# Moving three loads of values behind a later gate in a fused attention and feed-forward kernel

## The chip, the cores and the metric

The kernel runs on one core of one Trainium2 chip. The metric is the device time of one execution in microseconds (us); the lower the better. Runs of the kernel before give the time to compare with, and one further execution was taken with the hardware profiler.

## What is computed

The first stage is attention over a sliding window: eight batches, eight heads, 576 positions, heads of 64. A position sees the positions at most 32 away. The second stage takes the attention's output as 4608 tokens of 512 and runs a feed-forward block of width 2048 with a sigmoid-approximated GELU.

```python
scores = scale * np.matmul(q, k.transpose(0, 1, 3, 2))
mask = np.abs(pos[:, None] - pos[None, :]) <= window        # window = 32
attn = softmax(np.where(mask, scores, -1e9))
x = np.matmul(attn, v)                                      # (8, 8, 576, 64) -> (4608, 512)
h = x @ w_in                                                # (512, 2048)
g = h * (1.0 / (1.0 + np.exp(-1.702 * h)))
out = g @ w_out                                             # (2048, 512)
```

## The kernel before

The 4608 tokens are cut into 36 units of 128 and nine tiles of 512, four units to a tile. Units and tiles are counted from 0, so the third tile has the number t = 2, and while its first layer is computed, the attention of the units of the next tile is prepared. The whole order of work is written out by hand; each engine runs its own instructions strictly in the order in which the program issues them.

**Attention of a unit.** Queries and keys are loaded from memory into staging tiles (`qst`, `kst`, five buffers each, `load_kq`, L138), transposed by DMA from SP's queue (`T_dma`, L246, called by `turn`, L868) into `qT` and `kT`, multiplied to scores on the matrix engine (TensorE, called PE in the profile), turned into exponentials on ScalarE (ACT) and multiplied with a mask on VectorE (DVE; `band`, L360). The queries of a unit are shifted by 32 positions against its keys, so one half of the query rows needs the unit's own 128 values, and the other half the 128 values that begin 64 later.

**Values.** `load_v(u)` (L209) loads unit u's values into one of nine buffers `ve`, by a DMA issued from GpSimd (POOL). `odd_v(u)` (L224) makes the shifted copy `vo` of unit u, the "odd" values: one GpSimd copy takes the upper half of `ve` of unit u, a second the lower half of `ve` of unit u + 1. All loads of queries, keys and values are issued by GpSimd too, so the issues and the copies share one queue. `values_four(u)` (L407) multiplies the exponentials of four units with `ve` and `vo`, head after head, 32 heads in all (`pv` in the profile). `norm_four` (L425) divides by the sums on VectorE and sends each unit's result x to SP, which transposes it by DMA into `xT` of the next tile (L447).

**Feed-forward.** Both layers use Strassen-like schemes of seven products. `l1_group(t, n, ...)` computes group n of the four groups of the first layer of tile t; the products of the second layer of earlier tiles are kept in a list `l2` and filled in between. VectorE makes sums of the inputs (`xs`, L495 and L496, from `xT`) and of the results (`gs`, L507 to L510).

**The order around the change.** `back(t)` (L904) runs the four groups of tile t. At its start a group turns queries and keys on SP; in group 2 `values_four` and `norm_four` of the next tile's units take their place; the store of an output pair (L613, on SP) and the fill products are spread between. Behind each group stands a gate: GpSimd copies one element of the last sum `gs` into `seen` (L943), and as its queue is in order, it issues nothing further before VectorE has made that sum. Behind the gate GpSimd runs a row of the table `LOADS`, looked up by tile and group, else by group alone. In a row, `("v", 5)` loads the values of unit u + 5, `("kq", 9)` the queries of unit u + 9 and the keys of the unit after, and `("odd", 4)` makes the odd copies of unit u + 4, with u = 4t + 4, so u = 12 for the third tile. Values 17, 18 and 19 are one DMA each. `front(t)` (L877) stands between the tiles: the scores of the next tile's units, and the sums of x.

Of the kernel before, what the change touches and what calls it, by code (L numbers as in the profile page):

```python
# [26 lines left out]
class _Kernel:  # L27
# [689 lines left out]
    def opening(self):  # L717
# [95 lines left out]
        for u in (8, 9, 10, 11):  # L813
# [29 lines left out]
        self.x_T2(6, "t", act)  # L843
        self.do(self.l2, 5)

    LOADS = {(2, 1): [("kq", 8)], (2, 2): [("v", 5, 6, 7)], (2, 3): [("v", 8), ("kq", 9), ("odd", 4), ("kq", 10)],
# [25 lines left out]
    @staticmethod  # L872
    def do(fs, n=99):
        for _ in range(min(n, len(fs))):
            fs.pop(0)()
# [28 lines left out]
    def back(self, t):  # L904

        more = t + 1 < self.NT
        do, l2 = self.do, self.l2
        u = 4 * t + 4
        bands = [lambda i=i: self.band(u + i) for i in range(4)] if more else []
        dv = bands  # L910
        for n in range(4):
            for i in {2: ((4,), (5,), (6, 7), ()), 3: ((4, 5), (6, 7), (), (8,))}.get(t, ((5, 6), (7,), (), (8,)))[n]:
                self.turn(u + i)
            if t == 2:
                self.ahead("kq", *((17,), (18, 19), (), ())[n])
            if more and n == 2:
                self.values_four(u)
                self.norm_four(u, ("A", "C", "E"), (0, 1))
                do(l2, 1)

            key = n if more else ("last", n)
            if t == 2:
                key = ("first", n) if n < 2 else n
            share = dict(zip((1, 7, 2, 4), self.SHARES.get(key, (3, 3, 5, 5))))

            def fill(i):
                do(l2, share[i])
                self.l2eng = self.nc.scalar
                if i == 4 or more and (n, i) == (1, 7):
                    do(dv, 99 if i == 4 else 2)  # L930

            def side(i):
                if more and n == 2:
                    self.norm_four(u, (f"t{i}",), (2 + i,))
                else:
                    do(dv, 1)

            self.l1_group(t, n, fill, side)
            dv += self.g_sums(t, 2 * n, 2)
            if more and (t > 2 or n > 0):  # L940
                if u + n + 7 <= self.NU:
                    c = 2 * ((n - 1) % 4) + 1
                    self.nc.gpsimd.tensor_copy(self.seen, self.gs[t - (n == 0)][0:1, 2, c, 255:256])  # L943
                for what, *us in self.LOADS.get((t, n)) or self.LOADS[n]:
                    for i in us:
                        if what == "odd":
                            self.spread(u + i)
                        else:
                            self.ahead(what, u + i)
        return dv  # L950
# [136 lines left out]
```

## Time and profile before

| what | us |
|---|---|
| median of three timed runs | 279.52 |
| lowest and highest of them | 279.24, 280.18 |
| the profiled execution | 278.88 |
| its span, first to last instruction | 277.1 |
| TensorE busy in it | 265.1 |
| VectorE, ScalarE, GpSimd busy in it | 213.7, 196.1, 140.2 |

All times below that stand alone, such as 99.74, are us from the start of the span of the profiled execution. In a row of a timeline the first number is the start, the second the duration, then come the engine, the line of the kernel, the operation, what it writes and reads, and a count of merged instructions; a bracket tells how long the engine was idle before and what ended that. SPq is SP's queue of DMA issues. "To landing" is the time from a DMA's issue to the arrival of its data, as minimum, median and maximum. A row of a window has the window, its length, then for PE, weight loads, VectorE, ScalarE and GpSimd the busy us with the number of instructions, then the granted clock, the mean number of DMA engines' worth of queued work, and GB/s.

### The profile page before, as it was taken

What the parts mean: (1) busy time and instruction counts of PE and PEld (TensorE: products, weight loads), DVE (VectorE), ACT (ScalarE), POOL (GpSimd) and SP (SyncE); (2) the same over time, 40 slices, a digit from 0 to 9 for tenths busy, and PEclk for the clock granted to TensorE, in tenths of its full rate; (3) what the DMA queues carried; (4) which work ended last, traced back from release to release, by engine and by line L of the source; (5) the groups of instructions that cost most, each with busy time, mean ns of one, the idle gap of its engine ahead of it and who ended that gap; (6) DMA issues with size and microseconds to landing.
All of it is one profiled execution on the core that took longest, in us unless ns stands there. A gap on an engine that the chain in (4) does not pass through costs nothing.

```text
span 277.1 us, 8812 instructions
## 1 busy us (share of the span) xinstructions
PE 265.1 (96%) x3604; PEld 222.4 (80%) x3604; DVE 213.7 (77%) x496; ACT 196.1 (71%) x346; POOL 140.2 (51%) x218
## 2 busy tenths in 40 slices
PE   1989999999999999999999999999999999999994
PEld 1568556888788888888888888888888888888883
DVE  4655998987888788888878887888788878856621
ACT  2586985999896689669956985698569766577320
POOL 8995597999693189729642974294430000000000
PEclk9999999999999999999999999999999999999999
DMA  8999999999999999999999999999992023202033
GB/s 86 165 199 199 180 207 166 164 150 149 188 133 212 163 122 165 173 198 120 171 171 172 151 167 181 134 141 125 153 120 80 0 89 65 78 0 78 0 117 116
DMA packets 151353, 37.74 MB, mean 136 GB/s; under 512 B 138640, under 2 KB 146960, under 8 KB 151312
## 3 DMA queue, kind: packets, MB, share of 16 engines
q0 software_dynamic: 107200, 18.42, 95.4%
q1 hardware_dynamic: 43664, 18.23, 34.3%
q8 instruction: 28, 0.46, 0.7%
q10 hardware_dynamic: 448, 0.52, 0.6%
q14 instruction: 13, 0.11, 0.1%
HBM read 36.83 MB, written 9.44 MB: 167 GB/s over the span
## 4 chain that ended last, share of the span: by engine, by line
PE 93%; ACT 2%; DMA 2%; DVE 1%; issue 1%; POOLq 0%
PE o L71 41%; PE h L71 40%; PE sc L71 5%; PE pv L71 4%; DMA kq<-in_k_dram 2%; PE tp L180 1%; PE tp L259 1%; ACT kq L68 1%; PE tp L463 1%; ACT p L340 1%; DVE xn L398 1%; ACT L803 0%; PE tp L204 0%; DVE kq L68 0%; PE tp L451 0%
## 5 line engine op out<-in xcount | busy, mean ns | idle before, releaser
L579 ACT ACTIVATE g<-h 128x512 f16<-128x512 f32 x128 | 72.1, 598 | 37.9 <-PE h L71 31.6
L71 PEld LDWEIGHTS <-g 128*128 128x128 f16 x568 | 54.6, 98 | 7.7
L71 PE MATMUL h<-xs,a 128*128 128x256 f16 x384 | 57.6, 272 | 0.0
L71 PEld LDWEIGHTS <-a 128*128 128x128 f16 x512 | 49.7, 98 | 8.4 <-DVE xs L495 0.3
L71 PE MATMUL h<-xT,w 128*128 128x256 f16 (+1 forms) x352 | 53.6, 283 | 0.0
L71 PEld LDWEIGHTS <-w 128*128 128x128 f16 x480 | 46.0, 98 | 8.6
L71 PE MATMUL o<-w,g 128*128 128x256 f16 (+1 forms) x304 | 49.9, 284 | 0.0
L233 POOL COPY vo<-ve 64x264 int32<-64x264 int32 x71 | 35.6, 502 | 18.0 <-DMA ve<-in_v_dram 14.5
L71 PEld LDWEIGHTS <-gs 128*128 128x128 f16 x416 | 39.9, 98 | 5.3
L71 PE MATMUL o<-b,gs 128*128 128x256 f16 x280 | 43.3, 273 | 0.0
L71 PE MATMUL o<-b,g 128*128 128x256 f16 x264 | 38.6, 273 | 0.0
L592 DVE TENSOR_TENSOR h<-h,s 128x512 f32<-128x512 f32 x32 | 22.4, 699 | 18.8 <-PE h L71 18.2
L214 POOL DMA_DIRECT2D ve<-in_v_dram x39 | 33.2, 864 | 2.5 <-issue 1.2
L144 POOL DMA_DIRECT2D qst<-in_q_dram x35 | 28.2, 808 | 1.3 <-issue 0.9
L598 DVE TENSOR_TENSOR h<-h,s 128x512 f32<-128x512 f32 x32 | 22.3, 698 | 7.3 <-PE h L71 7.1
L144 POOL DMA_DIRECT2D kst<-in_k_dram x31 | 26.6, 861 | 1.4 <-DMA w<-in_moe_w_out_dram 1.4
L68 ACT COPY h<-h 128x512 f32<-128x512 f32 x32 | 18.8, 587 | 10.4 <-PE h L71 9.6
L293 ACT ACTIVATE p<-sc 128x512 bf16<-128x512 f32 x48 | 24.7, 623 | 0.3 <-PE sc L71 0.2
L943 POOL COPY seen<-gs 1x1 f16<-1x1 f16 x17 | 3.3, 196 | 36.9 <-DVE gs L510 36.9
L68 ACT COPY o_sb<-o 128x256 f32<-128x256 f32 (+1 forms) x25 | 11.7, 467 | 12.6 <-PE o L71 12.6
L68 ACT COPY s<-h 128x512 f32<-128x512 f32 x32 | 19.1, 598 | 0.8
L71 PE MATMUL h<-xs,w 128*128 128x256 f16 x128 | 19.2, 273 | 0.0
(101 smaller groups left out, 389.0 us busy)
## 6 DMA issues: line engine op xcount, KB each, us to landing
out_dram<-o_sb SPq DMA_DIRECT2D x33, 256.0 KB, 4.1
ve<-in_v_dram POOLq DMA_DIRECT2D x31, 128.0 KB, 6.5
kst<-in_k_dram POOLq DMA_DIRECT2D x25, 128.0 KB, 5.7
qst<-in_q_dram POOLq DMA_DIRECT2D x21, 128.0 KB, 5.2
w<-in_moe_w_out_dram POOLq DMA_DIRECT2D x4, 512.0 KB, 10.6
w<-in_moe_w_in_dram POOLq DMA_DIRECT2D x4, 256.0 KB, 8.5
w<-in_moe_w_in_dram POOLq DMA_DIRECT2D x2, 512.0 KB, 10.6
qst<-in_q_dram POOLq DMA_DIRECT2D x7, 96.0 KB, 5.8
```

What stands on the lines that cost most here:

```text
L68: (eng.copy if eng is self.nc.scalar else eng.tensor_copy)(out, in_)
L71: self.nc.tensor.matmul(out, lhsT, rhs, start=start, stop=stop, skip_group_check=True)
L144: self.nc.gpsimd.dma_start(t[off:off + n], src[b, :, s:s + n, :].rearrange("h s d -> s h d"))
L180: self.nc.tensor.transpose(tp[64 * (h % 2):64 * (h % 2) + 64, h // 2, x, :], src[:, 4 * i + h, at + x, :], self.ident[r, r])
L214: self.nc.gpsimd.dma_start(t[off:off + n, :, :self.D], self.v[b, :, s:s + n, :].rearrange("h s d -> s h d"))
L233: eng.tensor_copy(*((words(vo[64:128]), words(self.ve[u % 9][64:128])), (words(vo[0:64]), words(nxt)))[i])
L259: self.nc.tensor.transpose(tp[:, i, hp, :], src[:, 128 * hp:128 * hp + 128], self.ident)
L293: exps = [lambda eo=eo: self.nc.scalar.activation(p[:, eo].rearrange("k h s -> k (h s)"), sc[eo], AF.Exp, scale=self.scale) for eo in rang ...
L579: act.activation(g[:, f, 256 * half:256 * half + 256], bank.rearrange("p (i n) -> p i n", i=2), AF.Gelu_apprx_sigmoid)
L592: dve.tensor_add(e, b, s7)
L598: dve.tensor_add(c, b, s7)
L943: self.nc.gpsimd.tensor_copy(self.seen, self.gs[t - (n == 0)][0:1, 2, c, 255:256])
```

## The change

The row of the third tile's third group, (2, 2), becomes empty, and values 17, 18 and 19 go into the row of the fourth group, (2, 3), ahead of values 20. The lookup takes an empty row as a row: before, an empty one would have fallen through to the default of its group.

```diff
-    LOADS = {(2, 1): [("kq", 8)], (2, 2): [("v", 5, 6, 7)], (2, 3): [("v", 8), ("kq", 9), ("odd", 4), ("kq", 10)],
+    LOADS = {(2, 1): [("kq", 8)], (2, 2): [], (2, 3): [("v", 5, 6, 7, 8), ("kq", 9), ("odd", 4), ("kq", 10)],
              (3, 0): [("kq", 7), ("odd", 1, 2, 3), ("v", 5)],
              0: [("odd", 2), ("kq", 7), ("v", 5), ("odd", 3)], 1: [("kq", 8), ("v", 6)],
              2: [("odd", 4), ("kq", 9), ("v", 7)], 3: [("odd", 5), ("kq", 10), ("v", 8)]}
...
-                for what, *us in self.LOADS.get((t, n)) or self.LOADS[n]:
+                for what, *us in self.LOADS.get((t, n), self.LOADS[n]):
```

## The prediction, made before the change was run

> **What bounds the kernel now.** I read the page first, then the windows around the place of the change, then GpSimd's own order of time, and last the consumers of what GpSimd makes. On the page, the span, the busy times and the chain that ended last:
>
> ```profile
> span 277.1 us, 8812 instructions
> ...
> PE 265.1 (96%) x3604; PEld 222.4 (80%) x3604; DVE 213.7 (77%) x496; ACT 196.1 (71%) x346; POOL 140.2 (51%) x218
> ...
> PE 93%; ACT 2%; DMA 2%; DVE 1%; issue 1%; POOLq 0%
> ```
>
> The matrix engine is both the busiest engine and 93% of the chain. A busy share is an average, so the windows come next: I cut the stretch from the values of the third tile (87.30) in alternate pieces, from values to scores and from scores to values. The first column is the length, the second the matrix engine's busy time and its matmuls.
>
> ```profile
> 87.30:98.84 11.54, 11.54 (x162) 10.02 (x166) 9.44 (x25) 6.97 (x14) 4.57 (x6) 1.00 1.40 176
> 98.84:114.72 15.88, 15.88 (x232) 13.88 (x234) 13.69 (x29) 13.87 (x24) 13.10 (x21) 1.00 2.14 163
> 114.72:126.26 11.54, 11.54 (x162) 10.04 (x166) 9.49 (x25) 6.91 (x13) 6.13 (x10) 1.00 1.49 172
> 126.26:142.14 15.88, 15.88 (x232) 13.88 (x234) 13.58 (x29) 13.87 (x24) 9.77 (x17) 1.00 1.96 154
> ```
>
> This table decides most of the question. The first two pieces hold the loads that the change moves; the last two are the same work one tile later, where the change moves nothing. The lengths agree to 0.01 us (11.54 and 11.54, 15.88 and 15.88), with the same count of matmuls, a busy time equal to the length, and a clock of 1.00. So before the change no load, copy or transpose in this stretch makes the matrix engine wait, and a better place for a load has nothing to give back there. A change of GpSimd's order can only leave the time as it is, or add a wait.
>
> **The change part by part.** GpSimd's timeline, with the idle time ahead of an instruction in brackets:
>
> ```profile
> 95.72 0.18 POOL L943 COPY seen<-gs 1x1 f16<-1x1 f16 x1 [6.44 <-DVE gs L510]
> 96.19 2.63 POOL L214 DMA_DIRECT2D ve<-in_v_dram  x3 [0.29 <-issue]
> 99.74 0.24 POOL L943 COPY seen<-gs 1x1 f16<-1x1 f16 x1 [0.92 <-DVE gs L510]
> 100.25 0.88 POOL L214 DMA_DIRECT2D ve<-in_v_dram  x1 [0.27 <-issue]
> ...
> 103.42 1.18 POOL L233 COPY vo<-ve 64x264 int32<-64x264 int32 x2
> ...
> 107.78 0.89 POOL L144 DMA_DIRECT2D kst<-in_k_dram  x1
> 108.71 3.77 POOL L233 COPY vo<-ve 64x264 int32<-64x264 int32 x6
> ...
> 114.27 0.18 POOL L943 COPY seen<-gs 1x1 f16<-1x1 f16 x1 [0.97 <-DVE gs L510]
> ...
> 123.14 0.18 POOL L943 COPY seen<-gs 1x1 f16<-1x1 f16 x1 [5.23 <-DVE gs L510]
> ```
>
> The gate of the third group (the copy into `seen` at 95.72) stays, since it stands ahead of the row of loads and does not depend on it. The edit of the lookup adds no instruction: it lets an empty row count as a row. So nothing is added or removed; the three issues of values 17 to 19 are moved past one gate, the one at 99.74. That gate waits for VectorE and was already idle by 0.92 us before it, so it does not come earlier when the three issues are gone from ahead of it. From 100.25 on, everything in GpSimd's queue up to the last copy stands three issues later, which is 2.63 us: values 20, queries 21 and 22, keys 22 and 23, the two copies of odd unit 16, the gate of the next tile, queries 23, keys 24, and the six copies of odd units 17 to 19. Between 100.25 and the end of these copies (108.71 + 3.77 = 112.48) the queue has next to no gap (of its 2.78 idle us in the window from 98.84, 0.90 lie before the gate, 0.27 behind it and 0.97 before 114.27), so nothing there takes up the shift: the copies would end at 112.48 + 2.63 = 115.11 if each cost what it cost before.
>
> Do they cost the same? The six took 3.77 us, 0.63 each, beside VectorE's long mask products, the last of which end at 110.7. The row of these, and the group of all copies of this kind from 111.3 on, later in the same kernel:
>
> ```profile
> 109.20 1.49 DVE L367 TENSOR_TENSOR p<-p,mask 128x1024 bf16<-128x1024 bf16 x2
> ...
> L233 POOL COPY vo<-ve 64x264 int32<-64x264 int32 x29 | 13.6, 469 | 9.8 <-DMA ve<-in_v_dram 8.4
> ```
>
> At 0.469 us six take 2.8, and the end is 115.11 - 3.77 + 2.8 = 114.1. I keep both: 114.1 to 115.1, nearer the first, because at the new place the mask products are over. Who needs them? The products of values with odd units in the same phase, in the matrix engine's timeline (the first of 32, and the 25th, which is the first of unit 19, eight heads to a unit):
>
> ```profile
> 114.65 0.22 PE L71 MATMUL pv<-vo,p 128*64 128x65 bf16 x1
> ...
> 115.47 0.19 PE L71 MATMUL pv<-vo,p 128*64 128x65 bf16 x1
> ```
>
> Unit 19 is wanted at 115.47, 0.4 us after the later end and 1.4 after the earlier one. Units 17 and 18 are wanted at about 114.9 and 115.2, and their copies are done two pairs and one pair of copies sooner (0.94 to 1.26 us a pair). Cost on the path: nothing, on a cover of 0.4 to 1.4 us. This is the thinnest cover of the whole change.
>
> The copies also wait for their sources, and a copy that waits holds all issues behind it. Landing times, counted from the issue: values 20 today in the place that values 17 would take, and the five issues of an earlier back-to-back train:
>
> ```profile
> L214 POOL DMA_DIRECT2D ve<-in_v_dram x1: 881/881/881, 100.2 to 100.2; - x1
> DMA to landing us min/median/max: 4.1/4.1/4.1
> ...
> L214 POOL DMA_DIRECT2D ve<-in_v_dram x5: 705/922/933, 65.1 to 68.2; - x5
> ...
>   POOL vo L233: 2.3, 2
> ...
> DMA to landing us min/median/max: 5.1/6.9/7.4
> ```
>
> Odd unit 16 needs values 17. Its first copy would start at 103.42 + 2.63 = 106.05, its second 0.59 later, at 106.64. Values 17, issued at 100.25, land at 104.4 (by 4.1) to 107.7 (by 7.4). I take 104.4, because it is then the first load in the queue after an idle stretch, as in no other place of the train; no wait. Values 18 to 20 have over 10 us until their copies. The queue took the five-issue train without lengthening an issue (0.70 to 0.93 us), so a train of four values and what follows needs no price for issuing.
>
> The other road is SP's queue, which transposes the queries and keys in order, with a store and the next tile's transposes of x behind them. The load of keys 22 in two halves, SP's timeline, the landings of x, and who needs x:
>
> ```profile
> L144 POOL DMA_DIRECT2D kst<-in_k_dram x2: 715/719/723, 102.0 to 102.7; - x2
> ...
> DMA to landing us min/median/max: 5.9/6.6/7.3
> ```
>
> ```profile
> 110.13 1.19 SPq L250 DMA_TRANSPOSE kT<-kst  x1
> ...
> 115.42 1.21 SPq L250 DMA_TRANSPOSE kT<-kst  x1
> 116.73 1.69 SPq L613 DMA_DIRECT2D out_dram<-o_sb  x2
> 118.51 6.11 SPq L447 DMA_TRANSPOSE xT<-xn  x4
> ...
> 129.10 1.02 SPq L613 DMA_DIRECT2D out_dram<-o_sb  x2
> ```
>
> ```profile
> DMA to landing us min/median/max: 2.6/4.5/5.4
> ```
>
> ```profile
> 130.68 0.42 DVE L495 TENSOR_TENSOR xs<-xT 128x512 f16<-128x512 f16 x1
> ...
> 131.93 0.60 PE L71 MATMUL h<-xs,a 128*128 128x256 f16 x4
> ```
>
> The second half of keys 22, issued at 102.7, landed at 110.0, and their transpose followed at 110.13; four more, the store and the first transpose of x came behind it without a longer pause (five in 6.6 us from 110.13 to 116.73, 1.32 each). So this chain hangs on that landing, which with the same 7.3 comes 2.63 later. It moves as a whole: keys 24 at 118.05, the store at 119.4, the first transpose of x at 121.1. The four of x then follow at about 1.3 each (they took 6.11 with waits for the norm in between), the last issued at 125.0 and landed between 127.6 (2.6) and 130.4 (5.4). VectorE subtracts at 130.68, and its result, 0.42 later, is wanted at 131.93. Cost: nothing, with 0.3 us left for VectorE and 1.1 for the matrix engine in the worse sum. The transposed queries and keys themselves are first used by the scores at 126.26, 8 us after the last of them is issued, and the buffer of the delayed store is written again only after the store of 129.10.
>
> At the gate of 114.27 the queue was idle by 0.97; of the 2.63 at most 1.66 is carried past it, and the 5.23 idle before 123.14 takes that up. From the fifth tile on all stands as before.
>
> The sum: 0.0 us on the chain. The profiled execution took 278.88 for its span of 277.1, and stays there; the three timed runs have a median of 279.52, 0.64 above it, and I forecast that median: 279.5. I hold 0.3% (0.84 us) for about what a measurement of this kernel can tell from no change.
>
> **The rivals.** *Slower, by the odd copies.* If values 17 land late, the second copy of odd unit 16 waits, and everything behind it moves on. From the end of that copy (104.60) to the end of the six it is 7.88 us today. With 7.4 for the landing: 107.65 + 0.59 + 7.88 = 116.1, 0.65 past 115.47. If the copies wait besides as they did after the earlier train (2.3 us in two waits, row above), the end is 115.11 + 2.3 = 117.4, a wait of 1.9. Price 0.65 to 1.9, time 280.2 to 281.4. It decides from a landing of 6.8 us on (115.47 - 7.88 - 0.59 - 100.25). For it: loads late in a train land in about 7 us. Against it: values 17 open the train, and values 20 in that place took 4.1.
>
> *Slower, by the transposes of x.* Transposes issued among loads can land later, as query unit 20's did:
>
> ```profile
> L250 SPq DMA_TRANSPOSE qT<-qst x1: 1922/1922/1922, 102.6 to 102.6; - x1
> ...
> DMA to landing us min/median/max: 7.5/7.5/7.5
> ```
>
> If the last transpose of x, issued at 125.0, took that 7.5, it would land at 132.5, the subtraction end at 132.9, and the product of 131.93 wait 1.0: 280.5. It decides from a landing of 6.5 us on (131.93 - 0.42 - 125.0). Against it: the loads of the next row have landed by then. The Trainium skill, "DMA: Bandwidth & Descriptors", section "Queues, rings and completion order", speaks for it: a completion count is a strongly ordered write that lands only after earlier writes of that DMA engine, over all its queues. The 7.5 beside the train, against the 2.6 to 5.4 for x, agrees with that.
>
> *Faster, by a quieter place.* Values 17 to 19 are issued while the third tile's x is being transposed; without them those land sooner. The profiled execution shows no wait there:
>
> ```profile
> L447 SPq DMA_TRANSPOSE xT<-xn x1: 1234/1234/1234, 96.5 to 96.5; - x1
> ...
> DMA to landing us min/median/max: 4.5/4.5/4.5
> ```
>
> ```profile
> 103.26 0.42 DVE L495 TENSOR_TENSOR xs<-xT 128x512 f16<-128x512 f16 x1
> ```
>
> The last landed at 101.0, and its reader came at 103.26. Only if the timed executions lose there what the profiled one doesn't, up to the 0.64 between them, is there a gain: 278.9. The same section of the Trainium skill would favour it: each DMA engine goes round-robin over the queues with work, packet by packet. Here that could bring a landing forward, and 2.3 us of room already lies behind it.
>
> That the edit does nothing is excluded: with the new lookup the empty row is found and no default is taken, and every other row is as long as before.
>
> **How the numbers follow.** No change 0.64. Slower by the copies 0.17, of which 0.14 beyond 0.84; slower by x 0.07, of which 0.05 beyond it. Faster 0.12: its price of 0.64 stays inside the bound, and only with the scatter of the runs (279.24 to 280.18) does it pass it; I put 0.10 there, because a single profiled execution shows the timed ones only through this difference. What of a rival stays inside goes to no change: same 0.71, slower 0.19, faster 0.10. The range begins at 278.5 (278.9 less the 0.4 by which the runs lie off each other's median) and ends at 281.0, which takes in the copies' rival up to 1.5 of its 1.9.
>
> **What would show it.** Right: on GpSimd four loads of values in a row after the gate near 99.74, idle time before it of some 3.8 us, the six copies ending at 114 to 115.1, and pieces of 11.54 and 15.88 us as before. Wrong: the piece that ends with the values of the fourth tile longer than 15.88, with a wait on a copy or on values at its end (first rival), the one after it longer, with a wait for xs (second), or any piece shorter with fewer gaps (third).

## The result, and the profile after

The changed kernel takes 282.15 us (median of six runs, 280.82 to 284.01), against 279.38 for the kernel before in the six runs beside it (278.75 to 280.18): a ratio of 1.0102, 95% interval 1.006 to 1.0144. The forecast was 279.5 with a range up to 281.0. The change costs about 2.8 us. Two of the twelve timed runs of one kernel below (e4) were slow ones, 284.73 and 286.72, and are left out of its ratio.

The profiled execution took 281.35, 2.47 more than the one before. On its page, the span, the busy times and the chain:

```profile
span 279.6 us, 8812 instructions
...
PE 265.9 (95%) x3604; PEld 222.6 (80%) x3604; DVE 212.6 (76%) x496; ACT 196.2 (70%) x346; POOL 137.7 (49%) x218
...
PE 84%; DMA 5%; DVE 3%; POOL 2%; ACT 2%; issue 2%; POOLq 0%; DVEq 0%
```

As many instructions as before, but the chain now has 5% DMA, 3% VectorE and 2% GpSimd in it. The windows, cut at the same places of the program (0.4 us later here, a difference that stands already ahead of the first moved instruction):

```profile
87.72:99.26 11.54, 11.54 (x162) 10.02 (x166) 9.44 (x25) 6.97 (x14) 1.92 (x3) 1.00 1.69 183
99.26:115.14 15.88, 15.88 (x232) 13.88 (x234) 13.14 (x29) 13.87 (x24) 12.45 (x20) 1.00 1.63 132
115.14:126.93 11.79, 11.62 (x162) 10.10 (x166) 9.48 (x25) 6.91 (x13) 8.02 (x15) 1.00 2.04 183
126.93:144.68 17.75, 16.20 (x232) 13.71 (x234) 13.31 (x29) 13.95 (x24) 9.42 (x17) 1.00 1.92 172
```

The two pieces that hold the moved loads are as long as before. The loss lies in the two behind them, 11.79 for 11.54 and 17.75 for 15.88: 2.12 us, one tile later than the edit. Followed back from there, first the matrix engine's two waits and VectorE's:

```profile
116.24 0.19 PE L71 MATMUL pv<-vo,p 128*64 128x65 bf16 x1 [0.17 <-POOL vo L233]
...
134.32 0.61 PE L71 MATMUL h<-xs,a 128*128 128x256 f16 x4 [1.55 <-DVE xs L495]
```

```profile
133.83 0.43 DVE L495 TENSOR_TENSOR xs<-xT 128x512 f16<-128x512 f16 x1 [2.40 <-DMA xT<-xn]
```

The large one is the product that needs the sums of x; VectorE stood 2.40 for the last transpose of x. SP's queue shows why that was late, and GpSimd's and the landings why SP's was:

```profile
113.44 1.19 SPq L250 DMA_TRANSPOSE qT<-qst  x1
...
122.17 1.00 SPq L613 DMA_DIRECT2D out_dram<-o_sb  x2
123.26 5.53 SPq L447 DMA_TRANSPOSE xT<-xn  x4
```

```profile
100.15 0.24 POOL L943 COPY seen<-gs 1x1 f16<-1x1 f16 x1 [3.84 <-DVE gs L510]
100.62 3.50 POOL L214 DMA_DIRECT2D ve<-in_v_dram  x4 [0.22 <-issue]
104.08 0.91 POOL L144 DMA_DIRECT2D qst<-in_q_dram  x1
...
109.84 0.90 POOL L144 DMA_DIRECT2D qst<-in_q_dram  x1 [0.24 <-issue]
112.54 0.87 POOL L144 DMA_DIRECT2D kst<-in_k_dram  x1 [1.80 <-DMA ve<-in_v_dram]
113.45 2.74 POOL L233 COPY vo<-ve 64x264 int32<-64x264 int32 x6
```

```profile
L214 POOL DMA_DIRECT2D ve<-in_v_dram x4: 873/888/903, 100.6 to 103.2; - x4
...
DMA to landing us min/median/max: 3.3/6.3/9.0
...
L144 POOL DMA_DIRECT2D qst<-in_q_dram x1: 911/911/911, 104.1 to 104.1; - x1
...
DMA to landing us min/median/max: 9.3/9.3/9.3
```

GpSimd issues the four values and queries 21 at its old pace, 0.9 us each. They do not land at that pace: values 17 after 3.3 us, values 20 after 9.0, queries 21 after 9.3, at 113.4. Before, queries 21 landed 5.8 after issue and were transposed at 106.97:

```profile
L144 POOL DMA_DIRECT2D qst<-in_q_dram x1: 893/893/893, 101.1 to 101.1; - x1
...
DMA to landing us min/median/max: 5.8/5.8/5.8
```

```profile
106.97 1.19 SPq L250 DMA_TRANSPOSE qT<-qst  x1
```

Now SP transposes them at 113.44, and everything behind them in its queue moves: the transposes of x start at 123.26, for 118.51. The part of the chain that crosses this stretch names both:

```profile
103.21 9.03 DMA ve<-in_v_dram
...
127.59 6.16 DMA xT<-xn
133.83 0.44 DVE xs L495
```

What the DMA engines did meanwhile is in the last column of the windows, GB/s, and in the one before it. That one is a share of all 16 engines: the times of the packets added up, over the time of the 16, so 1.00 is as much as one packet on every engine throughout, and more than that means that packets overlap. It is not a count of engines. Before, and after:

```profile
96.00:99.00 3.00, 3.00 (x48) 2.49 (x49) 2.57 (x6) 1.70 (x4) 2.63 (x3) 1.00 0.90 124
99.00:102.00 3.00, 3.00 (x95) 2.55 (x86) 2.23 (x6) 2.97 (x5) 1.99 (x4) 1.00 2.02 139
```

```profile
96.00:99.00 3.00, 3.00 (x30) 2.63 (x27) 2.15 (x5) 1.41 (x4) 0.18 (x1) 1.00 0.67 131
99.00:102.00 3.00, 3.00 (x71) 2.46 (x68) 2.41 (x6) 2.97 (x5) 1.63 (x3) 1.00 0.23 49
```

Before, the three loads were under way in these windows, issued from 96.19 on. Now the engines have little to do from 99 to 102 (0.23, 49 GB/s, for 139 before), and the same bytes join the transfers that follow.

### The profile page after: what moved, and what is told of

Read it like the earlier page. It is cut to its first block, busy times and chain, and to the rows that moved or that the text cites. A ratio compares the mean times of both kernels' runs of the same rounds, so it can differ in the third digit from the quotient of the medians.

```text
span 279.6 us, 8812 instructions
## 1 busy us (share of the span) xinstructions
PE 265.9 (95%) x3604; PEld 222.6 (80%) x3604; DVE 212.6 (76%) x496; ACT 196.2 (70%) x346; POOL 137.7 (49%) x218
## 4 chain that ended last, share of the span: by engine, by line
PE 84%; DMA 5%; DVE 3%; POOL 2%; ACT 2%; issue 2%; POOLq 0%; DVEq 0%
PE h L71 37%; PE o L71 35%; PE sc L71 4%; PE pv L71 3%; DMA ve<-in_v_dram 3%; DMA xT<-xn 2%; PE tp L180 1%; PE tp L259 1%; ACT kq L68 1%; POOL vo L233 1%; PE tp L463 1%; POOL kq L155 1%; ACT p L340 1%; DVE xn L398 1%; POOL ve L214 1%
## 5 line engine op out<-in xcount | busy, mean ns | idle before, releaser
L233 POOL COPY vo<-ve 64x264 int32<-64x264 int32 x71 | 33.2, 468 | 16.7 <-DMA ve<-in_v_dram 11.5
```

The source lines that it names most:

```text
L233: eng.tensor_copy(*((words(vo[64:128]), words(self.ve[u % 9][64:128])), (words(vo[0:64]), words(nxt)))[i])
```

## The experiments

Two theories to begin with. Q: loads in a train land late, SP's in-order queue hands that on to the transposes of x, and the loss is the wait for the sums of x. V: the loss is at the values themselves, their copies and the products with odd units. The table gives what all kernels measured. The stretches are taken from starts in the matrix engine's timeline of each profiled execution, less the lengths of before: from the first product of the values of unit 16 to the first score of unit 20 (11.54 us before), on to the first product with sums of x (5.74), and on to the values of unit 20 (10.14). "x starts" is SP's first transpose of the fourth tile's x, less the shift of the gate near 99.74 in that execution.

| kernel | ratio to before, 95% | at the values | at the sums of x | rest | x starts |
|---|---|---|---|---|---|
| before | 1 | 0 | 0 | 0 | 118.5 |
| changed | 1.0102 (1.006 to 1.0144) | +0.26 | +1.72 | +0.15 | 122.9 |
| e1: one load moved | 0.9993 (0.9968 to 1.0018) | 0 | 0 | 0 | 119.8 |
| e2: two loads moved | 1.0017 (0.9998 to 1.0037) | 0 | 0 | +0.12 | 120.5 |
| e3: queries 21 first | 1.0097 (1.0063 to 1.0131) | +0.29 | +2.37 | +0.15 | 122.0 |
| e4: only queries 21 late | 1.0064 (1.0038 to 1.009) | 0 | +1.34 | +0.15 | 122.7 |
| e5: store from ScalarE | 1.0091 (1.0058 to 1.0125) | +0.73 | +1.86 | +0.16 | 122.7 |
| e6: unit 20 turned earlier | 1.0000 (0.9979 to 1.0022) | 0 | 0 | 0 | 120.5 |
| e7: values a gate earlier | 1.0000 (0.9987 to 1.0014) | 0 | 0 | 0 | 119.4 |
| e8: next loads later | 1.0025 (0.9998 to 1.0053) | +1.58 | +0.30 | +0.15 | 123.7 |

**One and two loads (e1, e2).** The row of the changed kernel, with one and with two loads of values moved:

```diff
-(2, 2): [], (2, 3): [("v", 5, 6, 7, 8), ...
+(2, 2): [("v", 5, 6)], (2, 3): [("v", 7, 8), ...        # e1
+(2, 2): [("v", 5)], (2, 3): [("v", 6, 7, 8), ...        # e2
```

> Only values 19 go behind the gate of the fourth group; values 17 and 18 stay where they were. Theory Q (loads in one train land about 1.4 us apart, so queries 21 land late, SP's in-order queue of transposes, store and x transposes moves on as a whole, and the product that needs the sums of x waits): one load more ahead of queries 21 lets them land some 1.5 to 2 us later, the last transpose of x lands before 130, and the room of about 1.4 us swallows it: 0.0 to +0.3 us against before. Theory V (the loss is at the values: three loads, their copies and the products with odd units each come later): a third of the loss of 2.8, about +0.9 us, with a wait at the values of the fourth tile.

> Values 18 and 19 go behind the gate, values 17 stay. Theory Q: the room is nearly used up; queries 21 land some 3 to 4 us later than before, the wait for the sums of x is 0 to 0.8 us: +0.0 to +0.8 us, far from two thirds of the whole because the loss starts only past a threshold. Theory V: two thirds of 2.8, about +1.9 us.

One load costs nothing that shows (-0.3 to +0.2%), two cost 0.0 to 0.4%, three 1.0%. That is a threshold, as Q has it, and no third per load, as V has it. In e2 VectorE has just begun to wait for x, and the matrix engine not yet:

```profile
132.40 0.43 DVE L495 TENSOR_TENSOR xs<-xT 128x512 f16<-128x512 f16 x1 [0.42 <-DMA xT<-xn]
```

**Queries 21 late, values untouched (e4).**

```diff
-(2, 2): [], (2, 3): [("v", 5, 6, 7, 8), ("kq", 9), ("odd", 4), ("kq", 10)],
-(3, 0): [("kq", 7), ("odd", 1, 2, 3), ("v", 5)],
+(2, 2): [("v", 5, 6, 7)], (2, 3): [("v", 8), ("kq", 10), ("odd", 4), ("kq", 11), ("kq", 9)],
+(3, 0): [("odd", 1, 2, 3), ("v", 5)],
```

> Values 17 to 20 stay exactly where they were before; instead queries 21 and keys 22 are issued last, behind queries 22, keys 23, the odd copies of unit 16, queries 23 and keys 24 (which are taken ahead of their gate for it). Theory Q: queries 21 land near 113 as in the changed kernel, SP's queue and the transposes of x are as late as there, and the loss returns without any value being moved: +1.3 to +2.8 us, as a wait for the sums of x. Theory V: values and copies are on time, so 0.0 us.

The loss returns with every value in its old place: +0.64%, and the same row as in the changed kernel, in SP's and the matrix engine's timelines.

```profile
113.57 1.22 SPq L250 DMA_TRANSPOSE qT<-qst  x1
...
123.09 5.52 SPq L447 DMA_TRANSPOSE xT<-xn  x4
```

```profile
133.74 0.61 PE L71 MATMUL h<-xs,a 128*128 128x256 f16 x4 [1.18 <-DVE xs L495]
```

V gave this kernel 0.0. So SP's queue is a road by which a late load costs time, and it is enough by itself for most of the loss.

**Queries 21 first (e3).**

```diff
-(2, 2): [], (2, 3): [("v", 5, 6, 7, 8), ("kq", 9), ("odd", 4), ("kq", 10)],
+(2, 2): [], (2, 3): [("kq", 9), ("v", 5, 6, 7, 8), ("odd", 4), ("kq", 10)],
```

> All of values 17 to 20 behind the gate as in the changed kernel, but queries 21 and keys 22 are issued ahead of them. Theory Q: SP can transpose queries 21 near 107 to 108 again, its queue then hangs on the last load (keys 24, landing near 117.5), the transposes of x start near 120 instead of 123.3, and the wait for the sums of x is gone: 0.0 to +0.5 us against before. Theory V: values 17 to 19 land still later than in the changed kernel, so the loss is at least as large, +2.8 us or more, with a longer wait at the values of the fourth tile.

Both missed. The loss stayed (+0.97%) but not where V put it: it is again the wait for the sums of x, 2.21 us, against 0.19 at the values. SP could turn queries 21 and keys 22 early, as planned, and then stood for queries 22:

```profile
108.55 1.19 SPq L250 DMA_TRANSPOSE kT<-kst  x1
115.86 1.20 SPq L250 DMA_TRANSPOSE qT<-qst  x1
```

```profile
109.25 0.40 POOL L233 COPY vo<-ve 64x264 int32<-64x264 int32 x1 [1.73 <-DMA ve<-in_v_dram]
```

Queries 22 stand behind the odd copies of unit 16 in GpSimd's queue, and the second of these now waited 1.73 for values 17. Q's mechanism held; what I had put at the head of the queue was not all that it could stall on.

**What makes the train land late (e6).** Queries 20 and keys 21 are transposed by SP in the middle of the train. In e6 that is done one group earlier, right behind the third tile's x:

```diff
-{2: ((4,), (5,), (6, 7), ()), 3: ((4, 5), (6, 7), (), (8,))}
+{2: ((4,), (5,), (6, 7), (8,)), 3: ((5,), (6, 7), (), (8,))}
```

> The changed kernel, with the two transposes of queries 20 and keys 21 issued on SP one group earlier, behind the third tile's transposes of x (near 98 to 101) instead of near 103 to 106 in the middle of the train of loads; these loads landed near 94. Theory C (the train lands at 2 to 3 us a load because two transposes and a store share the DMA engines with it): values 17 to 20 land by about 108 instead of 112, queries 21 near 109 instead of 113.4, SP's later queue comes forward by 3 us or more and the wait for the sums of x is gone: 0.0 to +0.6 us against before. Theory P (a train of loads lands at its own pace, whatever else runs): queries 21 still land near 113 and the loss stays near +2.8.

The loss is gone, with all four loads of values still in one train and GpSimd's order that of the changed kernel. Queries 21 land after 6.7 us instead of 9.3, and SP goes on at 110.58:

```profile
L144 POOL DMA_DIRECT2D qst<-in_q_dram x1: 923/923/923, 103.8 to 103.8; - x1
...
DMA to landing us min/median/max: 6.7/6.7/6.7
```

```profile
110.58 1.20 SPq L250 DMA_TRANSPOSE qT<-qst  x1
...
120.69 5.52 SPq L447 DMA_TRANSPOSE xT<-xn  x4
```

So the train lands late because of the two transposes in its middle, not by its length alone. How they delay it no run separates. The Trainium skill, "DMA: Bandwidth & Descriptors", section "Queues, rings and completion order", says that each DMA engine takes turns between the queues that have work, and the 9.3 against 6.7 agrees with that in direction. It need not be all: from 111 to 112, with values 20 and queries 21 still to land, the engines of the changed kernel moved 27 GB/s, where those of e6 moved 134 in that time. This pair of edits is no faster than the kernel before (ratio 1.0000): there was nothing left to win.

**What makes the last transpose of x late (e8).** In the changed kernel it landed 6.2 after its issue, where it took 2.6 before. The next gate's loads are issued just then. In e8 they go one gate later:

```diff
+(3, 2): [("odd", 4)],
+(3, 3): [("odd", 5), ("kq", 9), ("v", 7), ("kq", 10), ("v", 8)],
```

> The changed kernel, with the loads of the fourth tile's third group (queries 25, keys 26, values 23, issued at 124.9 to 127.5 beside the fourth x transposes) put off by one gate, into the fourth group's row. Everything up to 124 stays as in the changed kernel, so SP's queue is as late and the last transpose of x is issued near 127.6 as there. Theory L (those loads make the late transposes land late, 6.2 to 6.8 us after issue instead of 2.6 in the kernel before): the last one lands after 2.6 to 4 us, by 131.6, and the wait of 1.6 for the sums of x shrinks to under 0.5; what the new train of five loads costs the next tile comes on top and is read from its own place. Theory Q alone (the lateness of SP's queue is all of it): the last transpose still lands near 133.7 and the wait stays at 1.2 to 2.2.

The profiled execution does not show what L expects. SP's queue is later than ever (123.7), and GpSimd issues no load between 121.2 and 130.1; but the last transpose of x, issued at 128.1, holds VectorE until 133.3:

```profile
L447 SPq DMA_TRANSPOSE xT<-xn x2: 1194/1194/1195, 126.4 to 128.1; - x2
...
  DVE xs L495: 1.0, 1
...
DMA to landing us min/median/max: 2.8/2.8/2.8
```

```profile
133.37 0.43 DVE L495 TENSOR_TENSOR xs<-xT 128x512 f16<-128x512 f16 x1 [0.99 <-DMA xT<-xn]
```

The 2.8 belongs to the transpose issued at 126.4. For the last one no landing is recorded, and VectorE's wait dates it: 5.2 after its issue, between the 4 that L allows and the 6.2 of the changed kernel. The 0.30 at the sums of x is no gain either, because the matrix engine came there 1.58 later by another loss: in the time of before, its product with the sums starts at 133.8 here and at 133.9 in the changed kernel, for 131.9 before.

That other loss, 1.58, is at the values. Up to there the program is the changed kernel's, which lost 0.26 in its own profiled execution, so the same train can cost more or less. The issue of keys 24 was held 3.21 us, and the copies of odd units 17 to 19, behind it, came late for the products, three times:

```profile
113.56 0.88 POOL L144 DMA_DIRECT2D kst<-in_k_dram  x1 [3.21 <-DMA ve<-in_v_dram]
```

```profile
115.37 0.19 PE L71 MATMUL pv<-vo,p 128*64 128x65 bf16 x1 [0.19 <-POOL vo L233]
116.28 0.19 PE L71 MATMUL pv<-vo,p 128*64 128x65 bf16 x1 [0.46 <-POOL vo L233]
117.19 0.19 PE L71 MATMUL pv<-vo,p 128*64 128x65 bf16 x1 [0.47 <-POOL vo L233]
```

The twelve timed runs of e8 go from 279.12 to 281.98. Five are at 281.0 or above, the profiled one (281.04) among them; the other seven, at most 280.38, are below all six of the changed kernel (280.82 and up). The loss against before is 0.0 to 0.5%. So putting these loads off takes away most of the time lost, which speaks for L, but no profile shows a run in which it did, and what makes the last transpose land late stays open.

**The store out of SP's queue (e5).**

```diff
-self.nc.sync.dma_start(self.out[row:row + n, :], o[:n, i, :])
+(self.nc.scalar if (t, pr) == (2, 0) else self.nc.sync).dma_start(self.out[row:row + n, :], o[:n, i, :])
```

> The changed kernel, with the one store that stands on SP's queue between the last transposes of queries and keys and the transposes of the fourth tile's results x issued from ScalarE instead. GpSimd's order is untouched. Theory Q (SP's in-order queue hands the lateness on): the transposes of x start about 1.1 us sooner, and the wait for the sums of x shrinks from 1.6 by about that: +0.9 to +2.0 us against before instead of +2.8. Theory L (the last transpose of x lands late because the next gate's loads are in flight then, whenever SP issues it): it still lands near 133.7, and the loss stays near +2.8.

Inconclusive. The transposes of x were to start 1.1 us sooner and started 0.1 sooner, so the two theories were not set apart. At the values it lost 0.73, and 0.40 of that is a wait of the matrix engine for ScalarE that the changed kernel does not have, so issuing the store there may have a price of its own. The transpose of keys 24 ahead of them held SP for 2.14 us, for 1.21 in the changed kernel, and in this execution the first ones were issued later and further apart as well:

```profile
121.23 2.14 SPq L250 DMA_TRANSPOSE kT<-kst  x1
123.46 5.90 SPq L447 DMA_TRANSPOSE xT<-xn  x4
```

**The opposite move (e7).**

```diff
-(2, 1): [("kq", 8)], (2, 2): [], (2, 3): [("v", 5, 6, 7, 8), ...
+(2, 1): [("kq", 8), ("v", 5, 6, 7)], (2, 2): [], (2, 3): [("v", 8), ...
```

> The opposite move: values 17 to 19 are issued one gate earlier than before the change, behind queries 20 and keys 21 at 89 to 92, and the row of the third group is empty. Theory Q: nothing is late anywhere, and the matrix engine had no wait to lose: 0.0 us (within 0.3). A rival, by which any shift of these loads costs because they collide with other transfers (here with SP's transposes at 89 to 98, those of the third tile's x among them): the sums of x of the third tile, read at 103.3 with 2.3 us of room, come late: +0.5 to +2 us.

No change, as Q says. An empty row (2, 2) and a shift of these loads are harmless by themselves; only the later place costs.

## Why the prediction was wrong

**What bounds the kernel: right.** The windows without a gap said that no better place could win anything, and none did, neither e7 nor e6.

**"The sum: 0.0 us on the chain": wrong**, by three terms, and all three are landings that I had priced with those of the kernel before.

1. *"This chain hangs on that landing, which with the same 7.3 comes 2.63 later."* This step failed first. I moved the landings by the issue time of the three loads and nothing else. Queries 21 landed 9.3 us after issue, not the 5.8 that they took before, and keys 22 after 8.5 to 8.8. Instead of 121.1 the transposes of x start at 122.9 in the time of before. The move changed what every later load met: it left 99 to 102 with 49 GB/s and put the bytes in among the transposes of queries 20 and keys 21, and without those two in the middle (e6) the same train cost nothing. GpSimd's 2.63 us of issuing was not the price.

2. *"Landed between 127.6 (2.6) and 130.4 (5.4)."* The last transpose of x took 6.2, issued at 127.6 into the next gate's loads; before it had been issued at 123.4, ahead of them. I counted the room as 1.1 us against landings that stay as they were. With them, the later start alone would have brought the last x between 129.8 and 132.6 in the time of before, and the product 0 to 1.1 us late; it was 2.0 late, of which 0.26 had been lost at the values. That those loads make the landing longer is not shown: in e8 it still took 5.2.

3. *"A train of four values and what follows needs no price for issuing."* Keys 24 were held 1.80 us until values 20 had landed, and the six copies ended at 116.19, which is 115.8 in the time of before, instead of 115.1 at the latest. That is the +0.26 at the values. The copies themselves were as cheap as I took them (2.74 us for six).

**The rivals.** The second one, by the transposes of x, is what happened, with its place and its point: the wait is at the product of 131.93. I gave it 0.07 and 1.0 us; it was 1.72. The argument against it, that "the loads of the next row have landed by then", overlooked that the row after that one is issued then, from 124.86 to 127.5. The first rival had its place right and its cause wrong: values 17 landed in 3.3 us, sooner than I took, and the copies were late through the held issue behind them. That there is nothing to win by a quieter place was right.

**What stays open.** Queries 21 with three values ahead of them landed 6.3 us after issue (e2), with four 9.3: why the last load costs so much more than the two before is not settled; e6 shows only that two transposes in the middle are needed for it. Why the last transpose of x took 6.2 is open too.

## What to carry to other kernels

Before moving a load, look at what the DMA engines do at the old place and at the new one: three loads that cost nothing in their old place made queries 21, behind them, land 6.1 us later in the new one. Follow an in-order queue to its end, since a load that nobody needs soon can hold up a transpose that somebody does. And a margin counted with a landing time from the old place is no margin where the move also changes what the transfer meets.

## What the runs showed of the hardware

- Where the issue of a load was held for another load, it was for the one eight places earlier (keys 24 for values 20, held 1.80 in the changed kernel and 3.21 in e8). In the traces GpSimd's loads report their landing to eight semaphores in turn, and the held issue waits for the semaphore that keys 24 share with values 20. So it is the program's semaphores that hold it.
- A load of 128 KB takes 3.3 us to land at the head of a train and 9.3 as its fifth beside two transposes, 6.7 without them. The last transpose of x took 2.6 us to land before the change, issued at 123.4, and 5.2 to 7.5 in the seven kernels that issued it at 125.0 or later.
